# One read of nine rows, late in the first pass of a channel-attention kernel, issued in six parts

## The chip, the core and the metric

The kernel runs on one core of a Trainium2 chip. The metric is the device time of one execution, in microseconds (us). A profiled execution also leaves a trace: every instruction of the five engines, every DMA transfer with its issue and its landings (one from each of the 16 DMA engines that move its bytes), and every DMA packet. Engine names: PE is TensorE, DVE is VectorE, ACT is ScalarE, SP is SyncE; POOL (GpSimd) does next to nothing here. SP issues all reads, ACT issues all stores.

## What is computed

```python
def reference(x, w1, w2):            # x: 1 x 384 x 384 x 384, bf16
    xf = x.reshape(B, H * W, C)
    gap = jnp.mean(xf, 1)            # per channel
    gmp = jnp.amax(xf, 1)            # per channel
    h_a = relu(gap @ w1); h_m = relu(gmp @ w1)      # 384 -> 96
    scale = sigmoid(h_a @ w2 + h_m @ w2)            # 96 -> 384
    return x * scale[:, None, None, :]
```

The two relus are written as products with a comparison in the original. Every pixel must be seen once before `scale` is known, and once more to be multiplied by it.

## The kernel before

**Rows.** The 147,456 pixels are dealt to the 128 partitions, 1,152 each. One pixel of one partition has 384 channels of 2 bytes, 768 bytes; the text calls "a row" one such pixel in each of the 128 partitions. A row is 96 KB in all, and a read of nine rows moves 864 KB, 6,912 bytes in each partition.

**Two passes.** The first pass reads all 1,152 rows and makes the sum (PE) and the maximum (DVE) of every channel. SBUF can't hold all of them, so most are read again in the second pass, multiplied by `scale` on DVE (`multiply`, L436) and stored. Some stay in SBUF between the passes, 224 of them (seven groups of 32 rows, `PACKED`) in a packed form: four sets of 8 rows share the room of three (`pack`, L322 to L329), and ACT looks at every packed row with two squares (`test_one`, L301 and L302, five looks a group, 35 in all) to find whether a value was out of the range that packing can hold. Both squares write their bytes to `tested`, which lies in rows 0 to 3 of the tensor `rows`; the second square's sum goes to a column of row 4.

**One tensor for everything.** `rows` is one SBUF tensor of 5 + 280 rows in each partition. `held` is its first five rows, `body` the other 280. The places in `body` are laid out by hand (`HOME_AT`, `BETWEEN`, `PASSING`, `SLOTS`); a place that has been consumed is read into again. All instructions stand in the order of the code on their engines (a manual schedule), and the framework sets the semaphore waits from what each instruction reads and writes.

**The loop around the change** is the one over `steps` (L359 to L396). For every load, SP issues a read (L371), PE adds the rows to the sums (`sums`, L274), DVE takes the maximum into an accumulator of eleven rows (`maximum`, L340, in pieces of six and five rows); before the loads that follow a group of packed rows stand its tests and its packing. A read has three kinds of waits: the earlier user of its place must be done on DVE and on PE, and one of eight completion semaphores must be free. The semaphores go round: each transfer takes the next one, and waits until the transfer eight before it has landed.

The end of the first pass, in the order of the reads: two fills that pass through beside the last packed group (`BETWEEN[6]`, 25 and 23 rows), then `PASSING` with 16, 9, 22, 14 and 17 rows, `refill` with 8, `last_passing` with 17, the rows that stay (16, 15, 11, 11, 9, 11, 10, 8, 5) and the last ones (8, 2, 6, 5). The read of nine rows is `PASSING[1] = (78, 9)`: body rows 78 to 86. The code of the last packed group's tests and packing stands ahead of all of `PASSING`, so ACT may still be busy with it while SP issues these reads.

`FILLS` is a number of memsets of one element on DVE at the start of the kernel.

Of the kernel before, what the change touches and what calls it, by code (L numbers as in the profile page):

```python
# [63 lines left out]
PASSING = ((62, 16), (78, 9), (0, 22), (31, 14), (45, 17))  # L64
# [8 lines left out]
    + ((0, 30), (30, 30), (60, 30), (90, 30)) * 3 + ((0, 30), (30, 30), (60, 30), (90, 20))  # L73
)
FIRST_READ = (8, 16)
FILLS = 24

OPENING = (0, 24, (3, 4))
FIRST_PLACE = ((0, 8, (8, 8)), (0, 0, (8,)))
SECOND_PLACE = ((1, 0, (8, 9)), (2, 0, (10,)))  # L80
OTHER_PLACES = ((1, 17, (14,)), (2, 10, (24,)))
TEST_SCALE = 0.031187
SUM_TAIL = 4
MM_ROWS = 4

# [2 lines left out]
def kernel(  # L88
# [7 lines left out]
    nc = tc.nc  # L96
    P = nc.NUM_PARTITIONS
# [9 lines left out]
    xr = x.rearrange("b h w c -> (b h w) c")  # L107
    orr = out.rearrange("b h w c -> (b h w) c")

    def rows_of(ap, block):  # L110
        first, n = block
        return ap[first * P:(first + n) * P, :].rearrange("(p n) c -> p n c", n=n)
# [7 lines left out]
    def take(n):  # L120
        nonlocal at
        at += n
        return at - n, n
# [7 lines left out]
    passing_at, n_pass = at, TOT - at  # L131
    between = [[take(n) for _, n in group] for group in BETWEEN]
    passing = [take(n) for _, n in PASSING]
    last_passing = take(LAST_PASSING[1])
    assert at == TOT and sum(n for _, n in PLACES) == n_pass and held_block[1] == HELD_ROWS
    assert late_block[1] == LATE_ROWS and kept_block[1] == G and [sum(p) for p in STAYING] == [n for _, n in SLOTS]
# [27 lines left out]
    rows = nc.alloc_sbuf_tensor_at("rows", [P, HELD_ROWS + BODY_ROWS, C], BF16, offset=RING_BYTES).ap()  # L164
# [34 lines left out]
    nc.vector.memset(ones_bf, 1.0)  # L199
    for _ in range(FILLS):  # L200
        nc.vector.memset(small[0:1, 15:16], 0.0)
# [3 lines left out]
    nc.vector.memset(bank_a, 0.0)  # L205
    nc.vector.memset(test_bias, 4.5 * TEST_SCALE)
    nc.vector.memset(minus4, -4.0)
# [25 lines left out]
    for i in range(PACKED):  # L233
        if i in TOGETHER:
            lo = min(HOME_AT[i], D_AT[i % 2])
# [22 lines left out]
    loads = [st for st in steps if st[0] == "load"]  # L258
    tail_rows = sum(st[4] - st[3] for st in loads[len(loads) - SUM_TAIL:])

# [9 lines left out]
    def sums(rows, n, done, total):  # L270
        for k in range(0, n, MM_ROWS):
            g = min(MM_ROWS, n - k)
            for q in range(CQ):
                nc.tensor.matmul(  # L274
                    sum_ps[q * QP:q * QP + 1, 0:g * P],
                    lhsT=ones_bf[:, 0:1],
                    rhs=rows[:, k:k + g, q * P:(q + 1) * P],
                    start=(done + k == 0),
                    stop=(done + k + g == total),
                )  # L280

    def turn_sums():
        for r in range(MM_ROWS):
            nc.scalar.copy(out=s_sb[r % 2], in_=sum_ps[:, r * P:(r + 1) * P])  # L284
            nc.tensor.matmul(gsum_ps, lhsT=s_sb[r % 2], rhs=pick, start=(r == 0), stop=False)

    def tail_sums(rows, n, last):
        for k in range(n):
            for q in range(CQ):
                nc.tensor.matmul(  # L290
                    gsum_ps[:, q:q + 1], lhsT=rows[:, k, q * P:(q + 1) * P], rhs=ones_bf,
                    start=False, stop=(last and k == n - 1 and q == CQ - 1),
                )

    def test_one(rows, k):
# [3 lines left out]
        if len(rows.shape) == 3:  # L299
            out_ = out_.rearrange("p (r n) -> p r n", r=rows.shape[1])  # L300
        nc.scalar.activation(out=out_, in_=rows, func=ACT.Square, bias=test_bias, scale=TEST_SCALE)  # L301
        nc.scalar.activation(  # L302
# [3 lines left out]
    def test(i, what):  # L306

        if what == 2:
            test_one(high(part(i, 3), I8), 5 * i + 4)
            return  # L310
        n = G * C // 2
        a_b = homes[i][:, 0:2 * G, :].rearrange("p (r n) c -> p r (n c)", r=2).bitcast(I8)
        test_one(a_b[:, :, 2 * n * what + 1:2 * n * (what + 1):2], 5 * i + 2 * what)
        test_one(high(part(i, 2), I8)[:, n * what:n * (what + 1)], 5 * i + 2 * what + 1)

    def pack(i, half):
        n = G * C // 2
        span = slice(half * n, (half + 1) * n)
        for c in range(0, n, BANK):
            for r in range(4):  # L320
                for k, dt in enumerate((E4, E3)):
                    nc.tensor.matmul(  # L322
                        words[:, c:c + BANK], lhsT=weights[2 * r + k],
                        rhs=high(part(i, r), dt)[:, half * n + c:half * n + c + BANK],
                        start=(r == 0 and k == 0), stop=(r == 3 and k == 1),
                    )
        for r in (0, 1):
            nc.scalar.copy(out=high(part(i, r), U8)[:, span], in_=low(part(i, r + 2), U8)[:, span])  # L328
        nc.scalar.activation(  # L329
            out=part(i, 2).rearrange("p n c -> p (n c)").bitcast(U16)[:, span], in_=words,  # L330
            func=ACT.Copy, bias=32767.5,
        )

    def judge():
        nc.scalar.activation(out=test_copy, in_=tests[:, 0:NT], func=ACT.Copy, accum_out=test_sum)
        nc.scalar.copy(out=total, in_=test_sum)
        nc.tensor.matmul(bad_ps, lhsT=total, rhs=ones_bf, start=True, stop=True)

    def maximum(out_, in0, in1):
        nc.vector.tensor_tensor(out=out_, in0=in0, in1=in1, op=ALU.max)  # L340

    def turn_over(out_, rows):

        for r in range(LATE_ROWS):
            for q in range(CQ):
                nc.tensor.transpose(  # L346
                    out=out_[:, r, q * P:(q + 1) * P], in_=rows[:, r, q * P:(q + 1) * P], identity=ident_bf
                )
# [3 lines left out]
    def fold():  # L352

        n = folds[-1]
        h = n // 2
        maximum(acc[:, 0:h, :], acc[:, 0:h, :], acc[:, n - h:n, :])
        folds.append(n - h)

    done = turn = nth = 0  # L359
    for st in steps:  # L360
        if st[0] == "test":
            test(*st[1:])
        elif st[0] == "pack":
            pack(*st[1:])
        elif st[0] == "judge":
            judge()
        if st[0] != "load":
            continue
        _, block, rows, lo, hi = st
        m = hi - lo  # L370
        nc.sync.dma_start(out=rows, in_=rows_of(xr, block)[:, lo:hi, :])  # L371
        if nth < len(loads) - SUM_TAIL:
            sums(rows, m, done, TOT - tail_rows)
        else:
            tail_sums(rows, m, nth == len(loads) - 1)
        if nth == len(loads) - FOLD_BEFORE:
            fold()
        halves = HALVES if len(folds) == 1 else ((0, folds[-1]),)
        j = max(0, min(m, A - done))
        if j:  # L380
            nc.vector.tensor_copy(out=acc[:, done:done + j, :], in_=rows[:, 0:j, :])
        done += m
        if nth == len(loads) - SUM_TAIL - 1:
            turn_sums()
        while j < m:
            c, e = halves[turn % len(halves)]
            turn += 1
            e = min(e, c + m - j)
            maximum(acc[:, c:e, :], acc[:, c:e, :], rows[:, j:j + e - c, :])
            j += e - c  # L390
        if block == late_block:
            turn_over(late, rows)
        elif block == first_block:
            nc.vector.tensor_copy(out=kept_ps.bitcast(U32), in_=rows[:, 0:PSUM_ROWS, :].bitcast(U32))
            nc.vector.tensor_copy(out=kept_b.bitcast(U32), in_=rows[:, PSUM_ROWS:for_psum, :].bitcast(U32))
        nth += 1  # L396
# [222 lines left out]
```

## Time and profile before

| | us |
|---|---|
| three runs | 725.98, 726.03, 726.41; median 726.03 |
| the profiled execution | 725.41, of which the span from the first to the last instruction is 723.6 |
| DVE busy | 564.1 (78% of the span) |
| ACT busy | 349.8 (48%) |
| PE busy | 184.7 (26%) |
| bytes moved | 305.63 MB, 422 GB/s over the span |
| last read of the first pass has landed | 268.33 |
| first store issued | 277.00 |

The span has three stretches: the first pass to about 268 us, some 9 us in which `scale` is computed, and the second pass to the end. The chain of waits (the page's part 4) goes back from the last instruction to what released it, so it tells which engine or transfer set the end; a view of an engine in order of time gives start, length, and the idle time ahead of an instruction in brackets, with what ended it.

### The profile page before, as it was taken

Reading aid. Unit: us, or ns where it says so; the run is one execution under the profiler, and the core shown is the slowest. Engines: PE = TensorE matmul, PEld = TensorE weight load, DVE = VectorE, ACT = ScalarE, POOL = GpSimd, SP = SyncE. Lnnn points to the kernel's source line nnn. Section 1 sums busy time; section 2 is a strip of 40 time slices with the busy share of each in tenths; the row PEclk is TensorE's granted clock in tenths of the full one; section 3 lists DMA queues with packets and bytes.
Section 4 is the critical chain, followed back from the end, with each engine's and each line's share of the span. In section 5 each row is a group of like instructions: output and inputs, shape, how many; then the busy total and the mean of one; then the engine's idle time right before and its main releaser. Section 6 shows DMA issues by size and latency. Waiting matters only on the chain.

```text
span 723.6 us, 3882 instructions
## 1 busy us (share of the span) xinstructions
PE 184.7 (26%) x1363; PEld 74.2 (10%) x1363; DVE 564.1 (78%) x445; ACT 349.8 (48%) x251; POOL 0.7 (0%) x6
## 2 busy tenths in 40 slices
PE   5577475965867470000000000000000000001000
PEld 1222122322322140000000000000000000001000
DVE  5699899999999998797966554897888889495200
ACT  6999999997999200056230023806154442200000
POOL 0000000000000000000000000000000000000000
PEclk9888878896988555555555555555555555555555
DMA  9999999999999979999999999999999999999997
GB/s 380 434 438 435 417 442 427 429 430 432 431 426 428 426 312 356 400 433 431 433 431 431 434 428 431 434 430 435 430 429 432 437 432 430 430 433 439 442 426 339
DMA packets 20403, 305.63 MB, mean 422 GB/s; under 512 B 2624, under 2 KB 2976, under 8 KB 7200
## 3 DMA queue, kind: packets, MB, share of 16 engines
q1 hardware_dynamic: 13040, 192.14, 62.3%
q10 hardware_dynamic: 7344, 113.25, 36.6%
q8 instruction: 10, 0.16, 0.1%
q14 instruction: 9, 0.07, 0.0%
HBM read 192.14 MB, written 113.25 MB: 422 GB/s over the span
## 4 chain that ended last, share of the span: by engine, by line
DMA 63%; DVE 25%; issue 3%; PE 2%; ACT 1%; SPq 0%; DVEq 0%; ACTq 0%
DMA rows<-in_x_dram 40%; DMA out_dram<-rows 23%; DVE acc L340 16%; DVE rows L436 9%; PE words_ps L322 1%; ACT rows L328 0%; DVE acc L436 0%; SPq L371 0%; PE bank_a L274 0%; ACT rows L329 0%; ACT rows L487 0%; PE bank_a L430 0%; ACT scale_bc L431 0%; DVE small L424 0%; PE bank_a L423 0%
## 5 line engine op out<-in xcount | busy, mean ns | idle before, releaser
L436 DVE TENSOR_TENSOR rows<-rows,scale_bc 128x9216 bf16<-128x9216 bf16 (+9 forms) x56 | 230.9, 4164 | 91.2 <-DMA rows<-in_x_dram 90.0
L340 DVE TENSOR_TENSOR acc<-acc,rows 128x2304 bf16<-128x2304 bf16 (+4 forms) x227 | 245.0, 1154 | 13.9 <-DMA rows<-in_x_dram 13.6
L487 ACT COPY rows<-rows 128x1536 uint8<-128x1536 uint8 x28 | 41.3, 1476 | 204.2 <-DVE rows L436 144.8
L274 PE MATMUL bank_a<-rows,small 128*1 128x512 bf16 (+3 forms) x897 | 93.3, 466 | 80.9 <-DMA rows<-in_x_dram 76.1
L346 PE MATMUL words_ps<-ident_bf,acc 128*128 128x128 bf16 x24 | 2.7, 310 | 376.3 <-DVE acc L574 376.3
L301 ACT ACTIVATE rows<-rows 128x3072 uint8<-128x3072 int8 (+1 forms) x35 | 81.9, 2341 | 9.1 <-DMA rows<-in_x_dram 8.4
L302 ACT ACTIVATE rows<-rows 128x3072 uint8<-128x3072 uint8 (+1 forms) x35 | 82.0, 2344 | 1.1
L487 ACT COPY rows<-acc 128x1536 uint8<-128x1536 uint8 x42 | 60.5, 1473 | 18.2 <-DVE acc L473 17.7
L274 PEld LDWEIGHTS <-small 128*1 128x1 bf16 x897 | 30.6, 95 | 140.3 <-issue 118.2
L346 PEld LDWEIGHTS <-acc 128*128 128x128 bf16 x24 | 2.5, 144 | 376.7 <-DVE acc L574 376.7
L322 PE MATMUL words_ps<-rows,scale_bc 128*128 128x512 fp8e4 (+1 forms) x126 | 37.9, 414 | 9.2 <-ACT rows L329 9.2
L328 ACT COPY rows<-rows 128x1536 uint8<-128x1536 uint8 x28 | 39.7, 1468 | 0.4 <-PE words_ps L322 0.4
L322 PE MATMUL words_ps<-rows 128*128 128x512 fp8e3 (+1 forms) x126 | 35.8, 394 | 0.0
L468 DVE TENSOR_SCALAR rows<-rows 128x1536 uint16<-128x1536 uint16 x56 | 31.3, 560 | 1.9
L322 PE MATMUL words_ps<-rows,w_sb 128*128 128x512 fp8e3 x84 | 27.0, 405 | 0.0
L487 ACT COPY acc<-rows 128x1536 uint8<-128x1536 uint8 x14 | 20.5, 1466 | 0.0
L329 ACT ACTIVATE rows<-words_ps 128x1536 uint16<-128x1536 f32 x14 | 20.1, 1439 | 0.0
L322 PEld LDWEIGHTS <-scale_bc 128*128 128x128 bf16 x126 | 12.2, 103 | 30.2 <-issue 19.3
L322 PEld LDWEIGHTS <-rows 128*128 128x128 bf16 x126 | 12.9, 102 | 16.7 <-issue 3.3
L473 DVE SCALAR_TENSOR_TENSOR acc<-acc,rows 128x768 uint32<-128x768 uint32 x14 | 13.4, 959 | 0.5
L473 DVE SCALAR_TENSOR_TENSOR rows<-rows 128x768 uint32<-128x768 uint32 x14 | 13.4, 958 | 0.5
L284 ACT COPY w_sb<-bank_a 65x128 f32<-65x128 f32 x2 | 0.5, 261 | 24.5 <-PE bank_a L274 24.0
(61 smaller groups left out, 72.0 us busy)
## 6 DMA issues: line engine op xcount, KB each, us to landing
rows<-in_x_dram SPq DMA_DIRECT2D x16, 2880.0 KB, 25.4
out_dram<-rows ACTq DMA_DIRECT2D x15, 2880.0 KB, 22.8
rows<-in_x_dram SPq DMA_DIRECT2D x15, 2304.0 KB, 20.0
out_dram<-rows ACTq DMA_DIRECT2D x14, 2304.0 KB, 21.1
rows<-in_x_dram SPq DMA_DIRECT2D x4, 3072.0 KB, 31.8
out_dram<-rows ACTq DMA_DIRECT2D x2, 4608.0 KB, 46.7
rows<-in_x_dram SPq DMA_DIRECT2D x9, 768.0 KB, 16.7
rows<-in_x_dram SPq DMA_DIRECT2D x2, 3264.0 KB, 26.4
```

Source lines behind the costliest of these rows:

```text
L274: nc.tensor.matmul(sum_ps[q * QP:q * QP + 1, 0:g * P], lhsT=ones_bf[:, 0:1], rhs=rows[:, k:k + g, q * P:(q + 1) * P], start=(done + k == 0 ...
L301: nc.scalar.activation(out=out_, in_=rows, func=ACT.Square, bias=test_bias, scale=TEST_SCALE)
L302: nc.scalar.activation(out=out_, in_=out_, func=ACT.Square, bias=minus4, accum_out=tests[:, k:k + 1],)
L322: nc.tensor.matmul(words[:, c:c + BANK], lhsT=weights[2 * r + k], rhs=high(part(i, r), dt)[:, half * n + c:half * n + c + BANK], start=(r ...
L328: nc.scalar.copy(out=high(part(i, r), U8)[:, span], in_=low(part(i, r + 2), U8)[:, span])
L329: nc.scalar.activation(out=part(i, 2).rearrange("p n c -> p (n c)").bitcast(U16)[:, span], in_=words, func=ACT.Copy, bias=32767.5,)
L340: nc.vector.tensor_tensor(out=out_, in0=in0, in1=in1, op=ALU.max)
L346: nc.tensor.transpose(out=out_[:, r, q * P:(q + 1) * P], in_=rows[:, r, q * P:(q + 1) * P], identity=ident_bf)
L436: nc.vector.tensor_tensor(out=dst, in0=src, in1=scale_bc.unsqueeze(1).to_broadcast([P, n, C]), op=ALU.mult)
L468: nc.vector.tensor_scalar(out=u16(dst), in0=u16(src), scalar1=s1, scalar2=s2, op0=op0, op1=op1)
L473: nc.vector.scalar_tensor_tensor(out=u32(v), in0=u32(v), scalar=0x3F3F3F3F, in1=u32(m), op0=ALU.bitwise_xor, op1=ALU.bitwise_xor)
L487: nc.scalar.copy(out=dst, in_=src)
```

## The change

The read of `PASSING[1]` is issued as six reads of nine rows each: the 64 odd partitions, the 52 even ones from 0 to 102, and four times three partitions (104, 112, 120; 106, 114, 122; 108, 116, 124; 110, 118, 126). Together they are the same 128 partitions and the same 864 KB, to the same places. What PE and DVE do with the rows is unchanged. There is one memset less at the start (`FILLS` 24 to 23).

```diff
-FILLS = 24
+FILLS = 23
...
+PARTED = PASSING[1]
+PARTED_TO = 104
...
     passing = [take(n) for _, n in PASSING]
+    parted = passing[PASSING.index(PARTED)]
...
-        nc.sync.dma_start(out=rows, in_=rows_of(xr, block)[:, lo:hi, :])
+        parts = [slice(0, P)]
+        if block == parted:
+            parts = [slice(1, P, 2), slice(0, PARTED_TO, 2), *(slice(PARTED_TO + k, P, 8) for k in (0, 2, 4, 6))]
+        for some in parts:
+            nc.sync.dma_start(out=rows[some], in_=rows_of(xr, block)[some, lo:hi, :])
```

## The prediction

> **What bounds the kernel now.** First the page, for which engine and which stretch. DMA is busy throughout.
>
> ```profile
> DVE  5699899999999998797966554897888889495200
> ACT  6999999997999200056230023806154442200000
> ...
> PEclk9888878896988555555555555555555555555555
> DMA  9999999999999979999999999999999999999997
> ```
>
> The digits are tenths of 18.1 us slices. DMA has 9 nearly everywhere, so the whole span is near a transfer bound; the change stands in slice 11 (204 us), where DVE and ACT are full too. Next the table of stretches around it (PE, PEld, DVE, ACT, POOL busy, clock, DMA share, GB/s).
>
> ```profile
> 204.00:220.00 16.00, 12.34 (x87) 4.49 (x82) 16.00 (x17) 15.90 (x12) 0.00 (x0) 0.82 1.00 427
> 220.00:236.00 16.00, 12.54 (x90) 4.89 (x90) 15.71 (x16) 15.84 (x11) 0.00 (x0) 0.80 1.02 432
> 236.00:268.00 32.00, 18.21 (x145) 7.49 (x145) 31.13 (x31) 5.12 (x10) 0.00 (x0) 0.51 0.96 400
> ```
>
> From 204 to 236 DMA, DVE and ACT are all full; from 236 ACT is nearly free. DVE in order of time shows how tight it is:
>
> ```profile
> 227.57 13.11 DVE L340 TENSOR_TENSOR acc<-acc,rows 128x1920 bf16<-128x1920 bf16 x12 [0.29 <-DMA rows<-in_x_dram]
> 241.56 26.48 DVE L340 TENSOR_TENSOR acc<-acc,rows 128x1920 bf16<-128x1920 bf16 x26 [0.87 <-DMA rows<-in_x_dram]
> ```
>
> DVE waits 0.29 us and 0.87 us for reads and not again until 271.87, when the maximum is done. So the start at 241.56, set by the landing of `last_passing` at 241.47, fixes the end of the pass, and all that follows. Third, the landings of the reads around the change, each from the DMA view of its issue (KB, us to landing):
>
> ```profile
> rows<-in_x_dram SPq DMA_DIRECT2D x1, 1536.0 KB, 18.4
> ```
> ```profile
> rows<-in_x_dram SPq DMA_DIRECT2D x1, 864.0 KB, 18.1
> ```
> ```profile
> rows<-in_x_dram SPq DMA_DIRECT2D x1, 2112.0 KB, 11.1
> ```
>
> Issued at 202.04, 204.38 and 216.40, they land at 220.45, 222.49 and 227.48. The middle one is ours: when it is issued, 16 us of other reads are still ahead of it, which is the cover for anything that delays its issue. Behind the 16-row read that lands at 220.45 nothing else is queued.
>
> Last, ACT, since the built program names it (below):
>
> ```profile
> 229.85 2.86 ACT L301 ACTIVATE rows<-rows 128x3072 uint8<-128x3072 int8 x1
> 232.74 2.86 ACT L302 ACTIVATE rows<-rows 128x3072 uint8<-128x3072 uint8 x1
> 235.50 0.19 ACT L302 ACTIVATION_READ_ACCUMULATOR rows<-rows 128x1 f32 x1
> 235.59 2.83 ACT L328 COPY rows<-rows 128x1536 uint8<-128x1536 uint8 x2
> ```
>
> The third line is the last of the 35 tests; it ends at 235.69, and ACT had no wait since 175.44.
>
> **The change, part by part.** *A new wait.* In the built program the first part waits for DVE and PE as before, and, new, for ACT's semaphore at 118. Counting ACT's updates in program and trace alike, the 118th is that last L302, at 235.69. My reading: with a partition step of two the access is taken to overlap rows 0 to 3 of the same tensor, where the tests write. It has no data to protect, but the hardware obeys it. SP stands at 204.38 with all later reads behind it, and resumes at 235.69 instead. ACT can't be earlier: it is full, and waits for nothing that SP still has to issue.
>
> *What hides it.* SP loses 31.3 us; the queue covers 16.1 (204.38 to 220.45). DVE has work until it finishes the 16-row read (225.3 in its order of time). Then everything stands still.
>
> *The restart.* SP goes on 0.06 us after a release (chain of waits: 0.02 and 0.04), so part one is issued at 235.75. The first eight reads of the run, issued back to back, took 3.90 us, 0.49 each; with that the sixth part goes at 238.2 and the 22-row read at 238.7. Bounds for an issue: 0.33 (the lone one at 204.38) and 1.64 (L400, the slowest). Three-partition reads don't occur here; I keep the 0.49 of the same line. The first packets of the run came 1.0 us after their issue, so the 22-row read flows from 239.7. Before, it flowed on the earliest DMA engine from 220.07 (packet records). Shift there: 19.6 us.
>
> *The parts' data.* The run's first read, 384 KB into an empty queue, landed 3.5 us after issue, some 0.9 of it bytes at 427 GB/s; so 2.6 without bytes. The last part lands near 238.2 + 2.6 + 0.3 = 241.1. The parts' bytes take 2.04 us (220.45 to 222.49) if spread evenly, less than their issues, so their split costs nothing more; on one engine alone, twelve packets at 0.255 would be 3.1, still about that.
>
> *What comes back.* The sixteen landings of `last_passing` lie 3.2 us apart: DMA engines that also fetched instructions stay behind, and the last, hit at 27.1 and again at 234.4, is 1.1 behind the next. An empty queue lets all catch up. I allow 0.3 for the start and 1.4 for one later fetch (what the fetch cost that engine at 27.1), so 1.7 apart instead of 3.2: 1.5 less.
>
> *Sum.* `last_passing` lands at 241.47 + 19.6 - 1.5 = 259.6; DVE then has the same 30.3 us to 271.87. So +18.1. Check by DVE's idle time: from 225.3 to 241.1 it is 15.8; nine rows take 2.0, to 243.1; the 22-row read lands about 246.0, 2.9 idle instead of 0.29; its rows and the next three reads' are 13.0 of work, to 259.0, then 0.6 instead of 0.87. 15.8 + 2.6 - 0.3 = 18.1. The later waits on semaphores eight transfers back, and on places, shift with DVE and fall due over 6 us ahead of their bytes, as now.
>
> The other edits: one memset of one element less, and a few wait-only instructions on PE, DVE and ACT, stand at the start or beside waits; below 0.1 us either way. ACT's last look (L335) now also waits for the parts, at about 241; its result is due after 260. The second pass only starts later.
>
> The profiled execution took 725.41; 725.41 + 18.1 = 743.5. The median of the runs is 0.6 above it: **744.1**.
>
> [...] The landings show that a DMA read of 128 partitions uses all sixteen engines. [...]
>
> **Rivals.** *Balance, and no stall: not slower.* If ACT's semaphore stood at 118 before 204, the split would only move bytes between DMA engines. Should it take four packets (1.02 us) from the engine that is last, `last_passing` would land by 240.5, and DVE's wait of 0.87 would go: 725.1. Should it put four on that engine: 727.0. It decides when the wait is met by about 217, 3.5 us ahead of the empty queue. For it: the late engine is real. Against it: the count of 118 and the ACT rows. That is also the case in which the change does not do what is read here. Chance 0.06, 0.05 of it within 0.2%. [...]
>
> *An earlier test releases it.* If the wait meant the test before (226.5), 9.2 us less: 734.9. Against: the count. Chance 0.03, slower.
>
> *Dear parts.* At L400's 1.64 us for each of six, 6.9 more: 751.0. For: a strided set of partitions may cost SP more than a whole one. Against: L400 follows a transfer of 384 small runs, and the others of its line cost 0.33 to 0.56. Chance 0.06.
>
> **How the numbers follow.** The forecast has 0.85. Its own bounds: issues of 0.33 (-1.0), no fetch in the rest (-1.4), a quicker first landing (-0.5): 741.2; issues of 0.9 (+2.5), the late engine also the one with more packets (+1.0): 747.6. I widen to 740.5 to 748.0, which leaves out the cases named above, some 0.15. Within 0.2% (1.45 us) is about what a measurement of this kernel can tell from no change. Faster 0.01, same 0.05, slower 0.94.
>
> **What would show it.** SP's first part issued at 235.7 with a wait for ACT L302 of about 31 us; the slices of DMA empty between 221 and 237; DVE idle near 16 us in one piece, its next wait about 2.9; `last_passing` landing near 259.6, sixteen landings within 2 us; the first store at 295 instead of 277.00; ACT and the second pass unchanged in length. Wrong if SP issues the first part near 204, or if the six issues take much over 3 us.

## The result, and the profile after

The changed kernel takes 746.29 us (median of six runs, 745.57 to 746.65) against 726.12 us for the kernel before (six runs, 725.22 to 727.61). The ratio is 1.0275, with a 95% interval from 1.0262 to 1.0288. The forecast was 744.1 us, 18.1 us more than before. It is 20.2 us more: the sign and the mechanism are as forecast, and the size is about 2 us short.

The profiled execution took 746.18 us with a span of 744.4. In the new code the read is at L379 (before: L371), the maximum at L344 (L340), the two squares of a test at L305 and L306 (L301, L302).

First the 40 slices of the page, 18.6 us each:

```profile
DVE  6699899999991798978987343988888879496200
ACT  6999999997998000008440004534444260300000
...
DMA  9999999999972997999999999999999999999997
```

DMA's row has one new hole, a 7 and a 2 in slices 11 and 12, and DVE's row has a 1 right there. ACT's row stays at 9 and 8 through the hole. So DMA and DVE stand while ACT works.

The table of stretches (columns as before: PE, PEld, DVE, ACT, POOL busy, clock, DMA share, GB/s) gives the size:

```profile
204.00:220.00 16.00, 12.35 (x87) 4.57 (x87) 16.00 (x17) 15.90 (x12) 0.00 (x0) 0.82 0.94 400
220.00:236.00 16.00, 7.77 (x36) 2.87 (x35) 5.60 (x6) 15.84 (x11) 0.00 (x0) 0.71 0.00 1
```

Until 220 the stretch is nearly as before. By the packet records the last packets in the queue end at 220.1, and those of the next read start at 237.3. From 220 to 236 DMA moves 1 GB/s instead of 432, and DVE is busy for 5.6 us instead of 15.71. ACT's 15.84 us is the same to the hundredth.

What SP waited for, from its list of waits (total, times, longest):

```profile
SPq L379 <- DVE acc L344: 184.8, 27, 22.9
...
SPq L379 <- ACT rows L306: 31.3, 1, 31.3
```

Before, no line of the read's waits named the tests; now one wait of 31.3 us does. This is what released it, in ACT's order of time:

```profile
235.75 0.19 ACT L306 ACTIVATION_READ_ACCUMULATOR rows<-rows 128x1 f32 x1
```

It ends at 235.94, and SP issues the first part at 235.96. The 22-row read stands behind all six parts, and SP issues it at 240.44:

```profile
235.96 0.57 SPq L379 DMA_DIRECT2D rows<-in_x_dram  x1
...
240.44 0.34 SPq L379 DMA_DIRECT2D rows<-in_x_dram  x1
```

DVE in order of time then shows what the hole does to the end of the pass:

```profile
194.46 31.15 DVE L344 TENSOR_TENSOR acc<-acc,rows 128x1920 bf16<-128x1920 bf16 x30
242.37 2.03 DVE L344 TENSOR_TENSOR acc<-acc,rows 128x1920 bf16<-128x1920 bf16 x2 [16.77 <-DMA rows<-in_x_dram]
248.60 39.69 DVE L344 TENSOR_TENSOR acc<-acc,rows 128x1920 bf16<-128x1920 bf16 x38 [4.20 <-DMA rows<-in_x_dram]
```

DVE runs out of rows at 225.6, waits 16.77 us for the nine rows and 4.20 us for the 22 rows behind them. The 39.69 us behind that are merged into one line, as the idle time of 0.87 at `last_passing` has shrunk to 0.1: DVE is done with the rows ahead of it at 261.71, just when `last_passing` lands. The chain of waits still goes through that landing:

```profile
244.47 17.25 DMA rows<-in_x_dram
...
261.81 3.59 DVE acc L344 x4
```

Last, the DMA view of the issues between 235.9 and 240.6 (KB each, median us from issue to landing):

```profile
rows<-in_x_dram SPq DMA_DIRECT2D x1, 2112.0 KB, 8.1
rows<-in_x_dram SPq DMA_DIRECT2D x1, 432.0 KB, 3.9
rows<-in_x_dram SPq DMA_DIRECT2D x1, 351.0 KB
rows<-in_x_dram SPq DMA_DIRECT2D x4, 20.2 KB
```

The 2112 KB of the 22-row read are issued at 240.44 and land at 248.50, right ahead of DVE's restart at 248.60. `last_passing` lands at 261.71, and the first store is issued at 297.26 instead of 277.00, 20.26 us later. From there to the end it is 447.1 us (before: 446.6).

### The profile page after: what moved, and what is told of

The parts are those of the page before. It is cut to its first block, busy times and chain, and to the rows that moved or that the text cites. A ratio compares the mean times of both kernels' runs of the same rounds, so it can differ in the third digit from the quotient of the medians.

```text
span 744.4 us, 3892 instructions
## 1 busy us (share of the span) xinstructions
PE 188.3 (25%) x1363; PEld 74.6 (10%) x1363; DVE 564.2 (76%) x444; ACT 349.9 (47%) x251; POOL 0.7 (0%) x6
## 4 chain that ended last, share of the span: by engine, by line
DMA 63%; DVE 25%; issue 3%; ACT 2%; SPq 1%; PE 0%; DVEq 0%; ACTq 0%
DMA rows<-in_x_dram 45%; DMA out_dram<-rows 18%; DVE acc L344 16%; DVE rows L444 8%; ACT rows L305 1%; SPq L379 1%; ACT rows L306 1%; DVE rows L476 1%; ACT rows L332 0%; DVE acc L444 0%; ACT rows L333 0%; DVE acc L481 0%; DVE acc L476 0%; SPq L537 0%; PE bank_a L438 0%
## 5 line engine op out<-in xcount | busy, mean ns | idle before, releaser
L344 DVE TENSOR_TENSOR acc<-acc,rows 128x2304 bf16<-128x2304 bf16 (+4 forms) x227 | 245.1, 1156 | 34.0 <-DMA rows<-in_x_dram 33.7
L278 PE MATMUL bank_a<-rows,small 128*1 128x512 bf16 (+3 forms) x897 | 96.2, 476 | 97.4 <-DMA rows<-in_x_dram 92.9
L305 ACT ACTIVATE rows<-rows 128x3072 uint8<-128x3072 int8 (+1 forms) x35 | 81.9, 2340 | 9.1 <-DMA rows<-in_x_dram 8.4
L306 ACT ACTIVATE rows<-rows 128x3072 uint8<-128x3072 uint8 (+1 forms) x35 | 82.0, 2344 | 1.1
L476 DVE TENSOR_SCALAR rows<-rows 128x1536 uint16<-128x1536 uint16 x56 | 31.4, 560 | 1.9
L326 PEld LDWEIGHTS <-scale_bc 128*128 128x128 bf16 x126 | 12.3, 104 | 31.0 <-issue 20.2
```

Of the source, the lines that this page charges most:

```text
L278: nc.tensor.matmul(sum_ps[q * QP:q * QP + 1, 0:g * P], lhsT=ones_bf[:, 0:1], rhs=rows[:, k:k + g, q * P:(q + 1) * P], start=(done + k == 0 ...
L306: nc.scalar.activation(out=out_, in_=out_, func=ACT.Square, bias=minus4, accum_out=tests[:, k:k + 1],)
L326: nc.tensor.matmul(words[:, c:c + BANK], lhsT=weights[2 * r + k], rhs=high(part(i, r), dt)[:, half * n + c:half * n + c + BANK], start=(r ...
L476: nc.vector.tensor_scalar(out=u16(dst), in0=u16(src), scalar1=s1, scalar2=s2, op0=op0, op1=op1)
```

## The experiments

**Theory:** the wait for ACT's last test costs nearly all, and the pattern of the parts in the shared tensor is what brings it in. **Rival:** the six small transfers cost it themselves, in issues or in DMA time, whether they wait or not. Ratios are against runs of the kernel before on the same chip (725.74 us for e1 to e4, 725.66 for e5 to e8, 725.61 for e9).

### The wait alone

`e5_wait_alone` is the kernel *before*, with the read whole. It adds one copy of one element on ACT behind the last test. The copy reads the place into which the nine rows are to be read, so the whole read must wait for ACT.

```diff
+            if i == PACKED - 1:
+                nc.scalar.copy(out=tests[0:1, 2 * NT + 4:2 * NT + 5], in_=body[0:1, PASSING[1][0], 0:2].bitcast(F32))
```

> The kernel before, with the nine rows in one read, and one ACT copy of one element behind the last test that reads body row 78, so that this whole read must wait for ACT just as the first part does in the changed kernel. Theory A (the wait is the cause): SP waits some 31 us for ACT, the 22-row read lands about 245.5 instead of 227.48, 742 to 744 us. Theory B (the parts are the cause): 725 to 727.

Measured: 743.38 us, ratio 1.024 (1.0224 to 1.0256). SP's list of waits, and DVE in order of time:

```profile
SPq L373 <- ACT rows L311: 31.5, 1, 31.5
```
```profile
240.99 2.03 DVE L342 TENSOR_TENSOR acc<-acc,rows 128x1920 bf16<-128x1920 bf16 x2 [15.02 <-DMA rows<-in_x_dram]
246.05 13.12 DVE L342 TENSOR_TENSOR acc<-acc,rows 128x1920 bf16<-128x1920 bf16 x12 [3.03 <-DMA rows<-in_x_dram]
260.25 26.48 DVE L342 TENSOR_TENSOR acc<-acc,rows 128x1920 bf16<-128x1920 bf16 x26 [1.08 <-DMA rows<-in_x_dram]
```

The two idle stretches are there with one whole read, 15.02 and 3.03, near the forecast's 15.8 and 2.9. By the medians of the runs the wait alone, with no split, costs 17.7 us (743.38 against 725.66) of the change's 20.2. In the profiled executions the first store is issued at 295.70, 18.7 us later than before, where the changed kernel is 20.26 later. But the wait ended half a microsecond later in `e5` (its read is issued at 236.48, the first part of the changed kernel at 235.96), so with the same release it would be about 18.2.

### The parts without the wait

`e1_own_tensor` is the changed kernel with `held` and `body` as two SBUF tensors at the same addresses. In the built program, the parts then don't wait for ACT.

```diff
-    rows = nc.alloc_sbuf_tensor_at("rows", [P, HELD_ROWS + BODY_ROWS, C], BF16, offset=RING_BYTES).ap()
-    held, body = rows[:, 0:HELD_ROWS, :], rows[:, HELD_ROWS:HELD_ROWS + BODY_ROWS, :]
+    held = nc.alloc_sbuf_tensor_at("held", [P, HELD_ROWS, C], BF16, offset=RING_BYTES).ap()
+    body = nc.alloc_sbuf_tensor_at(
+        "rows", [P, BODY_ROWS, C], BF16, offset=RING_BYTES + HELD_ROWS * C * 2
+    ).ap()
```

> The changed kernel, with the first five rows (held) and the other 280 (body) as two SBUF tensors at the same addresses; the six parts and their strided partitions are unchanged. In the built program the wait for ACT is gone from the first part. Theory A (the stall is the wait for ACT's last test): SP issues the first part near 204.4, no empty slice of DMA, DVE's 16.8 us wait gone; 725 to 727 us, and if the split relieves the late DMA engine, up to 0.9 below the kernel before. Theory B (the six reads of part of the partitions are dear in themselves): still 730 to 746.

Measured: 727.43 us, ratio 1.0021 (1.0012 to 1.003), 0.4 us above the expected range. The first part is issued at 204.46, and SP's list has no line for the tests. The stall is gone: DVE's only two waits for reads in this stretch are these (the profiled execution itself took 730.35, the longest of the eleven):

```profile
229.41 13.12 DVE L346 TENSOR_TENSOR acc<-acc,rows 128x1920 bf16<-128x1920 bf16 x12 [2.04 <-DMA rows<-in_x_dram]
242.76 26.48 DVE L346 TENSOR_TENSOR acc<-acc,rows 128x1920 bf16<-128x1920 bf16 x26 [0.23 <-DMA rows<-in_x_dram]
```

So the tensor that the parts share with the tests brings in the wait. But 1.7 us stay by the medians of the runs. In this trace DVE waits 2.04 us for the 22 rows instead of 0.29, a cost of the split that the forecast had put at nothing, and 0.23 instead of 0.87 at `last_passing`. The first store is issued at 278.20, 1.2 us later than before; the rest of this one long execution lies in the second pass (450.4 us instead of 446.6).

`e8_two_tensors_whole` is the control: the kernel before with this edit alone.

> The kernel before with held and body as two tensors and nothing else, the control for e1 and e6: no time by either theory, within 0.3 us of the kernel before.

Measured: 725.83 us, ratio 1.0 (0.999 to 1.0009). Two tensors by themselves change nothing.

### The same split without a partition step

`e2_contiguous` keeps the one tensor and makes six parts of the same sizes from neighbouring partitions.

```diff
-            parts = [slice(1, P, 2), slice(0, PARTED_TO, 2), *(slice(PARTED_TO + k, P, 8) for k in (0, 2, 4, 6))]
+            parts = [slice(0, 64), slice(64, 116), *(slice(k, k + 3) for k in (116, 119, 122, 125))]
```

> The changed kernel with the six parts as runs of neighbouring partitions (0 to 63, 64 to 115, and four times three), so the same six sizes without a step. In the built program the first part does not wait for ACT. Theory A (the wait): near 204.4 for the first part, 725 to 727 us. Theory B (six reads of part of the partitions are dear): as the changed kernel, 740 to 746. If the step of the partitions itself cost DMA time, this one would be faster than the kernel with two tensors by over 0.5 us.

Measured: 728.62 us, ratio 1.0035 (1.0022 to 1.0049), 1.6 us above the expected range. The first part is issued at 204.50: in the same shared tensor there is no wait for ACT, so it is the step of the partitions that brings it, and not the number of parts. What is left without the wait is larger here, 2.9 us against 1.7 in `e1`, so parts of neighbouring partitions are dearer than the same sizes with a step.

### Two parts instead of six

`e3_two_parts` is the changed kernel with `parts = [slice(1, P, 2), slice(0, P, 2)]`.

> The changed kernel with two parts only, odd and even partitions; the first still waits for ACT in the built program. Theory A (the wait): first part at about 235.9, and only the four small issues and their 2.9 us (237.53 to 240.44 in the changed kernel) are saved: 743 to 744. Theory B (the many small parts): 727 to 731.

Measured: 744.59 us, ratio 1.0259 (1.0243 to 1.0274), 0.6 us above the expected range. SP's wait is 31.4 us, as with six parts. DVE:

```profile
240.65 2.03 DVE L344 TENSOR_TENSOR acc<-acc,rows 128x1920 bf16<-128x1920 bf16 x2 [15.25 <-DMA rows<-in_x_dram]
247.24 39.51 DVE L344 TENSOR_TENSOR acc<-acc,rows 128x1920 bf16<-128x1920 bf16 x38 [4.56 <-DMA rows<-in_x_dram]
```

The first store is issued at 295.71, with `e5` at 295.70. But the wait ended 0.7 us earlier here (the first part is issued at 235.77, `e5`'s read at 236.48). From that issue to the first store it is 59.2 us with the whole read, 59.9 with two parts and 61.3 with six. So behind the wait, where the queue is empty, odd and even partitions cost 0.7 us more than a whole read in these traces, and the 52 and the threes another 1.4. The medians have the same order (17.7, 18.9 and 20.2 us above before), but the intervals of `e5` and `e3` overlap.

### The wait at a later read

`e4_later_read` splits `PASSING[4]`, the 17 rows that are issued at 222.16 before (`PARTED = PASSING[4]`). The wait ends at the same time, but fewer reads stand behind it.

> The same split on another read, the 17 rows of the last entry of PASSING, which SP issued at 222.16 in the kernel before; the read of nine rows is whole. Its first part waits for the same ACT test. Theory A (the wait): SP stands from 222 to 235.9 instead of from 204, DMA is empty only from about 231, DVE misses these rows from 235.3 to about 243: some 8 us more than the kernel before, 733 to 736. Theory B (the parts' own cost): over 744, since these parts are larger.

Measured: 738.42 us, ratio 1.0174 (1.0158 to 1.0189), 2.4 us above the expected range. SP's waits and DVE:

```profile
SPq L379 <- ACT rows L306: 13.5, 1, 13.5
```
```profile
248.91 31.83 DVE L344 TENSOR_TENSOR acc<-acc,rows 128x2304 bf16<-128x2304 bf16 x31 [13.62 <-DMA rows<-in_x_dram]
```

The release is right: 13.5 us of waiting, from 222.2 to 235.75, in place of 31.3. The restart is what takes longer. The six parts, 1,632 KB or 3.9 us at 427 GB/s, are issued from 235.75 to 240.1 and the last lands at 248.63. Two things add up there, and the landings show both. The sixteen landings of the read behind the parts (`refill`, 768 KB) fall into three groups: three at 245.95 to 246.30, ten at 247.34 to 248.59 and three at 250.08 to 250.25. In the changed kernel the part of 64 left sixteen landings, the 52 thirteen and each three three. By these counts, if the threes all go to the same three engines, three DMA engines have four packets of the split rows, ten eight and three twelve, and that would give such groups; an even share is eight. And the packets are slow. The part of 52 has landed at 245.35, and the four small ones land at 245.94, 247.05, 247.72 and 248.63: 3.3 us for four packets more on the engines that are last. At 0.488 us each, the usual time of this size before, four packets take 2.0.

### What the parts cost in themselves

The packet records of `e1` show packets of the 22-row read, not split itself, at 0.760 us in the mean, against 0.629 for all 128 of them before. A tenth of them take 1.258 or more, twice the usual time. So the parts slow a transfer beside them. Three kernels look for what brings it about, all without a wait for ACT. `e6_odd_even_no_wait` is `e1` with odd and even partitions only; `e7_halves` is the changed kernel with `parts = [slice(0, 64), slice(64, P)]`; `e9_five_even` is `e1` with `parts = [slice(1, P, 2), *(slice(k, P, 8) for k in (0, 2, 4, 6))]`.

> Two tensors as in e1, so no wait for ACT, and two parts only, odd and even partitions: four packets on each of the 16 DMA engines in either part. It leaves out the uneven shares and the four small issues. If the 1.7 us that e1 lost come from packets at half speed (DMA engines that write partitions outside their own share and meet there), about half remains: +0.5 to +1.2. If they come from the uneven shares and the small parts: 0 within 0.3.

> Two parts only, partitions 0 to 63 and 64 to 127; no wait for ACT in the built program. In e2 the first part of this shape had most of its 6,912-byte packets at 0.48 us and more instead of 0.262. If engines that write into one half of the partitions get in each other's way, these packets are slow again and it costs as much as or more than odd and even parts: +1 to +3. If only the uneven shares cost: 0 within 0.3.

> Two tensors (so no wait for ACT), and five parts: the 64 odd partitions, and four times the 16 even partitions that lie eight apart (0, 8, ..; 2, 10, ..; 4, 12, ..; 6, 14, ..). No part has 52 or 3 partitions, so all sixteen DMA engines should have one packet of each small part. Theory 1 (the 1.7 us that are left of the six parts without the wait come from the uneven shares of 52 and 3 partitions): time as before, -0.3 to +0.5 us, the packets of 6,912 bytes at 0.262 us throughout, the 22-row read landing within 0.5 us of before, DVE's wait for it below 0.8. Theory 2 (they come from small parts as such, whose DMA engines write to partitions that others write to at the same time): +1.0 to +3.0, packets of the parts and of the reads beside them up to twice as long, DVE's wait for the 22-row read 1.5 to 3. The issues (some 0.55 to 0.65 each, five of them) are hidden in both by the 16 us of queued reads.

| kernel | parts | us | ratio (95%) | mean packet of the 22-row read |
|---|---|---|---|---|
| before | 128 | 726.03 | | 0.629 |
| `e6` | 64 odd, 64 even | 725.46 | 0.9994 (0.9985 to 1.0003) | 0.629 |
| `e9` | 64 odd, four times 16 even | 727.00 | 1.0019 (1.001 to 1.0028) | 0.741 |
| `e1` | 64 odd, 52 even, four times 3 | 727.43 | 1.0021 (1.0012 to 1.003) | 0.760 |
| `e7` | lower 64, upper 64 | 728.40 | 1.0035 (1.0021 to 1.0049) | 0.757 |
| `e2` | 64, 52, four times 3, neighbours | 728.62 | 1.0035 (1.0022 to 1.0049) | 0.788 |

The wait for the 22 rows, in `e9` and then in `e7`:

```profile
229.42 13.12 DVE L346 TENSOR_TENSOR acc<-acc,rows 128x1920 bf16<-128x1920 bf16 x12 [2.40 <-DMA rows<-in_x_dram]
```
```profile
230.17 13.12 DVE L344 TENSOR_TENSOR acc<-acc,rows 128x1920 bf16<-128x1920 bf16 x12 [2.73 <-DMA rows<-in_x_dram]
```

`e6` has no such line, and not one slow packet; DVE runs on to `last_passing`:

```profile
194.05 46.33 DVE L346 TENSOR_TENSOR acc<-acc,rows 128x1920 bf16<-128x1920 bf16 x44
241.38 26.48 DVE L346 TENSOR_TENSOR acc<-acc,rows 128x1920 bf16<-128x1920 bf16 x26 [1.00 <-DMA rows<-in_x_dram]
```

By what was expected of it, `e6` spoke for the uneven shares and the small parts as the cause of `e1`'s rest. `e9` takes the uneven shares out. Each of its parts left sixteen landings, so every DMA engine has the same share, and still it costs 1.4 us and its packets are slow. Uneven shares are therefore not needed for the cost. Nor are small parts: `e7` has two parts of 64 like `e6`, and costs 2.7 us. These two differ in which partitions a part holds (and in the two tensors, which cost nothing by `e8`), so that decides between slow packets and none. The parts of `e9` are also smaller and more numerous than those of `e6`; no run separates that.

The two halves show it best: in `e7`, the 128 packets of the two parts take 0.432 us in the mean, against 0.262 for every one before. The two parts of 64 in `e6` left the 22-row read's packets at 0.629 us, those in `e7` brought them to 0.757. What it is in these sets of partitions that slows the packets, no run shows, nor why the 52 and the threes are as slow as `e9`'s sets (0.760 and 0.741).

## Why the prediction was right, and where it was short

- **The bound, and the path through `last_passing`.** Right before the change. After it, the forecast let DVE wait three times, the last time 0.6 us for `last_passing`. It waits twice, and then 0.1 us there. Two paths now end together: the landing of `last_passing` at 261.71, and DVE's work behind the 22-row read that landed at 248.50. That they do so within 0.1 us is chance. (The maximum is done at 273.44 before, three instructions later than the 271.87 of the forecast; they shift alike and change no sum.)
- **The wait for ACT's 118th update.** Right: 31.3 us of waiting, forecast 31.3. That the step of the partitions in a shared tensor brings it in was a reading; `e1` (two tensors) and `e2` (no step) each take the wait away, and both show it.
- **ACT's end.** It came at 235.94 instead of 235.69, a quarter of a microsecond.
- **What hides it.** Right: DMA was empty from 220 to 236, and DVE ran out at 225.6 (forecast 225.3). `e4` agrees in direction: a wait of 13.5 us costs 12.7 and not 20.2, though more than the 8 expected of it.
- **The six issues.** This step failed in size. The forecast took 0.49 us for each, 2.95 in all, and let the 22-row read go at 238.7. From the first part at 235.96 to the 22-row read at 240.44 it is 4.48 us, with 0.57 us for the 64, 0.89 for the 52, 0.65 to 0.69 for each three, and the rest between them. That is 1.5 us more, the largest part of the 2.2 us by which the first store came later than forecast. The mean of 0.75 lies within the bounds that were put to it (0.33 to 0.9), near the upper one. But six issues of much over 3 us were named as a sign of being wrong, and in this term the prediction was.
- **"Their split costs nothing more."** This failed too, by about 0.8 us here. The 22-row read takes 8.06 us from its issue to its landing, where the forecast had 7.3. Its packets took 0.750 us in the mean instead of 0.629, eight of them to an engine, about 1.0 us. In `e5`, with the same wait and a whole read, they took 0.632, and in `e3`, with two parts, 0.689, so the parts bring most of it and not the empty queue. Without the wait, where 16 us of queued reads hide the issues, slow packets are what is left, and the kernel takes 1.7 us longer (`e1`).
- **The lag of the late DMA engine.** Right as a mechanism: the sixteen landings of `last_passing` lie 1.45 us apart instead of 3.2 (forecast 1.7). Before, the last of them came 1.2 us behind the next, where the forecast read 1.1. It earned 1.1 us and not 1.5 (next point).
- **The sum.** `last_passing` landed at 261.71, forecast 259.6; the first store came 20.26 us later, forecast 18.1. By the packet records the 22-row read flows from 241.42, forecast 239.7: a shift of 21.35 us instead of 19.6, from ACT's end and the issues. Of this 1.1 us came back by `last_passing`, forecast 1.5. On DVE's path, ACT's end 0.25, the issues 1.5 and the slow packets 0.8 make 2.5 at the 22-row read (248.50 against 246.0). DVE makes up about half a microsecond of it, as it waits 0.1 instead of 0.6 at `last_passing`.
- **The rivals.** *No stall* did not happen, and `e1` shows that it would have been 727.4. That is near the 727.0 of worse balance, but by luck: `e9`, with even shares, takes 727.0 as well, by slow packets. *An earlier test* fell with ACT's row at 235.75. Its price was misread: the test before the last ended at 229.82 in the kernel before (a row of 0.19 us at 229.63), and 226.5 is the end of the one ahead of that. So it would have been 5.9 us less, 738.2, and not 734.9. *Dear parts* named the term that was short, but at 1.64 us an issue; it was 0.75 in the mean of the six.
- **The shares of the DMA engines.** The forecast allowed twelve packets on one engine, moved four in *no stall*, and had an engine "with more packets" (+1.0) in its upper bound. No run shows these terms themselves: before, the reads of 128 partitions left sixteen landings each, and the landings have no engine's number. In the changed kernel the 64 partitions left sixteen landings, the 52 thirteen and each three three, with one earlier record ahead of the thirteen and of the threes. Shares of four, eight and twelve packets fit these counts and the three groups of landings in `e4`. The packet of 0.255 did not hold: by the packet records the 128 packets of the parts took 0.351 us in the mean, up to 1.113. Still the last part landed 2.59 us after its issue (239.66 to 242.25), no more than the 2.9 of the forecast.

## What to carry to other kernels

Before a transfer is cut into parts with a step, read in the built program what each part waits for: an access with a step may be taken to overlap a neighbour in the same tensor (31.3 us of waiting here), and one wait on the issuing queue costs its length less what is queued ahead of it, and the restart of an empty queue on top (in `e5` 31.5 us of waiting, 15.9 of them covered, leave 15.6, and the first store came 18.7 later). Here a tensor of its own for what others write took such a wait away (`e1`) at no cost (`e8`, 725.83 us against 725.66). The parts of a split can slow the transfers beside them as well, depending on the partitions that each holds (a packet of the 22-row read took 0.757 us in `e7`, 0.629 in `e6`). So a split that is to balance DMA engines is to be tried first alone, as odd and even partitions, which cost nothing here behind a full queue (`e6`, 725.46 us against 725.66).

## What the runs showed that was not expected

- How long SP takes to issue a read depends on its partitions. Most whole reads beside the parts took 0.33 to 0.46 us, 64 partitions 0.55 to 0.58 with a step of two or without (`e6`, `e7`). For 52 it was 0.89 with a step of two and 0.59 without, for three 0.65 to 0.69 with a step of eight and 0.24 to 0.27 without (`e2`). So for the 52 and the threes much of it is the step, and for the 64 none of it.
- A packet of one size is not of one duration. Before, all 128 packets of the 22-row read took 0.629 us; beside the parts they took up to 2.28 us in the changed kernel, and up to 1.53 in `e1`, though the read was not split itself.
- After an empty queue the first packets are slow as well, without any split: in `e5` the nine rows' packets took 0.315 us in the mean (up to 0.941) instead of 0.262.
